# Heads before places within a tile of the output's features, and a new table by slot, in a gated mix of two memory-augmented attentions

## The chip, the cores and the metric

The kernel runs on one core of one Trainium2 chip. The metric is the device time of one execution in microseconds (us). A change of 0.5% or less is treated as no change.

## What is computed

Two independent attentions, A and B, read the same input x (2048 tokens, 640 features), and a gate per token mixes their outputs. Each has 32 heads of 20 features and runs over 4 segments of 512 tokens. Within a segment it is causal softmax attention; between segments it keeps a memory per head (a 20 x 20 matrix M and a vector z). The part of the reference that matters:

```python
def ref(x, wq, wk, wv, wo, beta):          # H = 32, Dh = 20, N = 4, L = 512
    q, k, v = heads_and_segments(x @ wq), heads_and_segments(x @ wk), heads_and_segments(x @ wv)
    g = sigmoid(beta)                      # one number per head
    for s in range(N):
        p = softmax(q[s] @ k[s].T * Dh ** -0.5 + causal_mask)
        a_dot = p @ v[s]
        a_mem = (phi(q[s]) @ M) / (phi(q[s]) @ z + 1e-6)
        o[s] = g * a_mem + (1 - g) * a_dot
        M, z = M + phi(k[s]).T @ v[s], z + phi(k[s]).sum(tokens)
    return concat_heads(o) @ wo

t = sigmoid((x * gate_w).sum(-1))          # one number per token
out = t * ref(x, A...) + (1 - t) * ref(x, B...)
```

All tensors are float32. A product is made of three products with each operand split into a high and a low part (names ending in h and l, or `hi` and `lo`).

## The kernel before, in words

**Tiles and slots.** The work is cut into 8 tiles t: segment t // 2 of attention A (t even) or B (t odd). A tile has 8 groups of 4 heads, so there are 64 groups, and a slot i for each; two more slots end the program. Beside the groups runs the "fill": the projections q, k and v in five blocks of 128 features, and the output product with wo of the tile before.

**Order.** The order on every engine is made when the program is built. A planner keeps a clock, gives each step a cost in us (`put` for an engine, `dma` for a transfer, which all go out on SyncE, the queue SP), and emits a step when its inputs are due by these costs. For a transfer the due time is the issue (0.44), 0.9 us, its own cost, and `lat`. On the chip each engine works its queue in that order and waits where the planner was wrong. The table `RULES` has a row for many of the slots: the order in which the score tiles S (for the row maxima) and T (for the exponentials) are laid between the fill, the share of the slot that they take, and limits on when late steps may come in. A slot without a row keeps the rules of the slot before it.

**A group.** S tiles: TensorE writes a score tile into a bank (line 1205) and VectorE scans it for the row maxima (line 1192, tile `mx`). The maxima are transposed and go into the rows of `qst` beside the queries. T tiles: scores again with the maxima taken off (line 1295), exponentials on ScalarE (line 1287), the mask on GpSimd (line 1288). Then the product with v (line 1315); the result has 32 rows per head: 20 places of the output, and from row 20 on the sum of the exponentials. There are 8 banks, and TensorE waits when the next one is still being read.

**Normalisation.** For tiles 0 to 6 the result of each group is copied (line 1345) and sent to a tensor in memory, `dots[t]` (line 1360), with row 32 h + r for head h. When all eight groups of a tile are there, the tile is read back in another order: five loads of 128 x 512, one per block k of 128 output features (`mix`, line 1434), and one of the sums of exponentials, each repeated for four rows (`reciprocals`, line 1392). VectorE makes the gate over the sum (lines 1375 and 1380); then each of the five is weighed on VectorE (line 1425) or GpSimd (line 1426), whichever has less planned work. For t > 1 the memory part is added (line 1493). High and low parts are made (lines 1416, 1418 and 1419), and the output product may begin. Tile 7 is normalised on the chip.

**The order of features.** A block k of 128 output features holds the places 4 k to 4 k + 3 of all 32 heads. Before, the place is the outer index within a block and the head the inner one. The same order is needed in three other places: the rows of wo, which are brought into it by two passes through memory at the start (`mix_weights`: `wrow`, then `wmix`, line 569; read at line 550), the output tile `O` of the memory part (`by_head`, line 702, written by `mem_unit`, line 898; its columns are transposed at line 921, in `turn`), and `own`, which sums a head's gate over its rows (line 336). For tile 7 the head is outermost over the whole row, before and after.

Of the kernel before, what the change touches and what calls it, by code (L numbers as in the profile page):

```python
# [42 lines left out]
def tile_gated_mix_infini_attn(  # L43
# [282 lines left out]
    def small_tiles():  # L326
# [10 lines left out]
        for i in (2, 3):  # L337
            nc.gpsimd.tensor_tensor(out=own, in0=own, in1=ident[:, H * i:H * i + H], op=ALU.add)
# [1031 lines left out]
    def lanes_of(t):  # L1370
        return dots[t].rearrange("(h r) n -> r h n", r=32)
# [417 lines left out]
```

## Time and profile before

| | |
|---|---|
| median of 3 runs | 1110.36 us (1109.23 to 1113.66) |
| the profiled execution | 1116.47 us, its span 1114.7 us |
| TensorE busy | 1040.0 us, 93% of the span |
| VectorE, ScalarE, GpSimd busy | 772.2, 661.7, 595.4 us |
| mean granted TensorE clock | 0.959 |
| transfers | 241.99 MB, mean 217 GB/s, 149223 packets, 12592 of them under 512 B |

Busy times overlap, so they don't add up to the span. PE is TensorE, PEld its weight loads, DVE VectorE, ACT ScalarE, POOL GpSimd, SPq the queue from which transfers are issued. A row of a group reads: line, engine, operation, written from read, shape, count, busy time, mean of one in ns, idle time just before and what ended it. "DMA row<-dots" is a transfer that writes a row buffer from `dots`. In the chain that ended last a transfer counts from its issue until what waited for it went on.

### The profile page before, as it was taken

The page shows a single profiled execution, that of the slowest core. Times are in us where ns is not written, and L with a number is a line of the kernel's source. Part 1 is how long each engine was busy: PE and PEld are TensorE (multiplying, and loading weights), DVE is VectorE, ACT ScalarE, POOL GpSimd, SP SyncE. Part 2 cuts the span into 40 slices and gives each one's busy share as a digit, 9 for nine tenths or more (in the row PEclk, how much of TensorE's full clock was granted, in tenths as well). Part 3 has the DMA queues.
Part 4 walks back from the last instruction along what each step waited for, and adds up shares of the span by engine and source line. Part 5 has one row for each costly group of instructions (what it writes and reads, how often), then busy time and mean ns, then how long its engine had stood idle before and what let it go on. Part 6 is the DMA issues. An engine that isn't in the chain of part 4 may idle for free.

```text
span 1114.7 us, 30803 instructions
## 1 busy us (share of the span) xinstructions
PE 1040.0 (93%) x11260; PEld 884.7 (79%) x11260; DVE 772.2 (69%) x2605; ACT 661.7 (59%) x1347; POOL 595.4 (53%) x1033
## 2 busy tenths in 40 slices
PE   9899998799979999879997999986999889997998
PEld 7889877678868888778886888886888777876776
DVE  4687776567867678666776877865657677776764
ACT  5376665576645666546764567653766446664572
POOL 4356455556437656465644456455565345654461
PEclk9999999899989999889999999998999889998999
DMA  7999886688667877638776578764866669767522
GB/s 238 293 294 279 263 261 212 185 262 274 230 209 204 260 258 236 204 100 256 233 214 199 165 252 246 249 208 114 252 201 217 197 166 290 221 187 249 143 88 72
DMA packets 149223, 241.99 MB, mean 217 GB/s; under 512 B 12592, under 2 KB 45520, under 8 KB 149072
## 3 DMA queue, kind: packets, MB, share of 16 engines
q1 hardware_dynamic: 149072, 240.03, 70.3%
q8 instruction: 89, 1.46, 0.5%
q14 instruction: 62, 0.51, 0.2%
HBM read 150.83 MB, written 94.65 MB: 220 GB/s over the span
## 4 chain that ended last, share of the span: by engine, by line
PE 73%; DMA 18%; issue 3%; DVE 3%; POOL 1%; ACT 1%; SPq 1%; POOLq 0%; DVEq 0%; ACTq 0%
PE bank L771 42%; PE bank L1315 11%; DMA row<-dots 7%; PE bank L1205 6%; PE bank L1295 6%; DMA row<-in_xT_dram 3%; PE bank L961 3%; DMA wst<-wmix 2%; PE bank L881 2%; PE bank L921 2%; DMA qd<-row 1%; DVE bank L1192 1%; PE bank L1230 1%; DMA kst<-kd 1%; DMA wst<-in_b_wv_dram 1%
## 5 line engine op out<-in xcount | busy, mean ns | idle before, releaser
L1192 DVE CUSTOM_DVE_ANT_0 bank<-bank,tri 128x128 f32<-128x128 f32 (+3 forms) x1024 | 475.1, 521 | 166.9 <-PE bank L1205 130.4
L771 PE MATMUL bank<-row,wh 64*128 64x512 f32 x2308 | 501.7, 404 | 0.2
L1287 ACT ACTIVATE p<-bank 128x512 f32<-128x512 f32 x574 | 314.8, 600 | 149.9 <-PE bank L1295 125.9
L1288 POOL TENSOR_SCALAR_AFFINE_SELECT p<-p 128x256 f32<-128x256 f32 (+1 forms) x574 | 211.6, 377 | 262.4 <-ACT p L1287 243.9
L771 PEld LDWEIGHTS bank<-row,wh 64*128 64x128 f32 x2308 | 322.2, 187 | 11.1 <-DVE O L898 0.6
L771 PE MATMUL bank<-row,wl 64*128 64x512 f32 x1154 | 304.3, 404 | 0.0
L541 POOL TENSOR_TENSOR wl<-wst,wh 128x640 fp32r<-128x640 f32 x115 | 180.1, 1568 | 82.2 <-ACT wh L539 81.6
L771 PE MATMUL bank<-wvh,row 64*128 64x320 f32 x1280 | 199.1, 329 | 8.9 <-DVE row L1493 4.6
L1205 PE MATMUL bank<-kst,qst 60*128 60x128 f32 (+3 forms) x1024 | 185.4, 322 | 19.2 <-DVE row L737 7.0
L1295 PE MATMUL bank<-qst,kst 62*128 62x128 f32 (+3 forms) x1024 | 181.4, 323 | 12.3 <-DVE mx L1192 9.6
L771 PEld LDWEIGHTS bank<-row,wl 64*128 64x128 f32 x1154 | 180.4, 188 | 5.3 <-issue 0.8
L771 PEld LDWEIGHTS bank<-wvh,row 64*128 64x128 f32 x1280 | 161.7, 196 | 12.5 <-DVE row L1493 4.9
L1205 PEld LDWEIGHTS bank<-kst,qst 60*128 60x128 f32 x1024 | 138.3, 190 | 29.4 <-DVE row L737 7.3
L1295 PEld LDWEIGHTS bank<-qst,kst 62*128 62x128 f32 x1024 | 135.0, 189 | 21.4 <-DVE mx L1192 11.0
L1315 PE MATMUL bank<-p,vst 128*32 128x512 f32 (+3 forms) x1904 | 146.5, 431 | 0.5 <-POOL p L1288 0.4
L1192 DVE DVE_READ_ACCUMULATOR2_ANT mx<- 128x1 f32 x1024 | 144.4, 141 | 0.0
L1315 PEld LDWEIGHTS bank<-p,vst 128*32 128x32 f32 x1904 | 58.9, 111 | 87.7 <-issue 65.2
L539 ACT CAST wh<-wst 128x640 fp32r<-128x640 f32 x119 | 87.0, 739 | 57.5 <-DMA wst<-wmix 19.5
L771 PE MATMUL bank<-wvl,row 64*128 64x320 f32 x640 | 110.0, 322 | 0.0
L771 PEld LDWEIGHTS bank<-wvl,row 64*128 64x128 f32 x640 | 87.4, 195 | 0.1
L1345 ACT COPY row<-bank 128x512 f32<-128x512 f32 x60 | 35.3, 589 | 68.9 <-PE bank L1315 63.9
L516 POOL TENSOR_TENSOR wvl<-wst,wvh 128x640 fp32r<-128x640 f32 (+1 forms) x48 | 64.0, 1336 | 21.3 <-ACT wvh L513 20.9
(117 smaller groups left out, 1233.2 us busy)
## 6 DMA issues: line engine op xcount, KB each, us to landing
qst<-qd SPq DMA_DIRECT2D x128, 240.0 KB
kst<-kd SPq DMA_DIRECT2D x128, 240.0 KB
qd<-row SPq DMA_DIRECT2D x40, 512.0 KB
kd<-row SPq DMA_DIRECT2D x40, 512.0 KB
dots<-row SPq DMA_DIRECT2D x56, 256.0 KB
wst<-wmix SPq DMA_DIRECT2D x35, 320.0 KB
row<-dots SPq DMA_DIRECT2D x42, 256.0 KB
qd<-row SPq DMA_DIRECT2D x40, 256.0 KB
```

What stands on the lines that cost most here:

```text
L516: put("G", 0.77 * n, lambda: nc.gpsimd.tensor_tensor(out=wl[:, a:b, :], in0=w3, in1=r32(wh[:, a:b, :]), op=ALU.subtract), end, prio=4)
L539: put("A", 0.625, lambda: nc.scalar.copy(wh, w3), lambda: put(lo_eng, lo_cost, lambda: lo.tensor_tensor(out=wl, in0=w3, in1=r32(wh), op=AL ...
L541: lambda: lo.tensor_tensor(out=wl, in0=w3, in1=r32(wh), op=ALU.subtract), end, prio=3), prio=6)
L771: return nc.tensor.matmul(bank_of, lhsT=w[ROWS[half]], rhs=x_[ROWS[half]], start=start, stop=stop)
L961: return nc.tensor.matmul(b[:, :nh * E1], lhsT=r32(pkn[ROWS[half], P * n:P * (n + 1)]), rhs=vst[t % 2][ROWS[half], n, LO[m] * E1:(HI[m] + ...
L1192: put("D", w / 960.0 + 0.105, lambda: nc.vector.tensor_tensor_reduce(out=sc[:, off:off + w], in0=sc[:, off:off + w], in1=tri[:, L - w:], s ...
L1205: lane_ops[half].append((mm(w), lambda pair=pair, qb=qb, off=off, w=w, r=r, sc=sc: nc.tensor.matmul(sc[:, off:off + w], lhsT=q[r, pair, P ...
L1287: put("A", 0.483, lambda: nc.scalar.activation(pt, sc, AF.Exp, scale=SCALE), lambda: (bank.give(sc), put("G", 0.15 + 0.105 * len(todo), la ...
L1288: "G", 0.15 + 0.105 * len(todo), lambda: nc.gpsimd.affine_select(out=blocks, in_=blocks, pattern=[[0, len(todo)], [1, P]], base=0, channel ...
L1295: lane_ops[half].append((mm(w), lambda pair=pair, kb=kb, off=off, w=w, r=r, sc=sc: nc.tensor.matmul(sc[:, off:off + w], lhsT=k[r, pair, P ...
L1315: nc.tensor.matmul(po[32 * j:32 * j + 32, P * kb:], lhsT=vst[t % 2][:, kb, h * E1:h * E1 + 32], rhs=pts[i, n, f][0][:, off:off + w], start ...
L1345: either(0.483, lambda: nc.scalar.copy(r32(oT), po), 0.605, lambda: nc.vector.tensor_copy(r32(oT), po), end, 2)
```

## The change

Within a block of 128 features the head becomes the outer index and the four places the inner one. So the three kinds of transfer (`dots` loads, sums of exponentials, `wmix` writes) have 32 heads outermost and four places within; the bytes and their number are the same. The memory part writes `O` in runs of four places, `own` is made with a fill and two selections, and the table of rules is replaced as a whole. Lines between the table and `own` stand three earlier than before, lines behind 900 two later (1434 is 1436 now).

```diff
@@ RULES @@
-        2: "TSTSTSTSTS 1.039 2.38 0.30 8 2.8 1.6 0.76",
-        4: "TSTTSSTSTS 1.042 2.38 0.30 4 0.0 1.6 1.57",
...
+        1: "TSTSTSTSTS 0.984 2.38 0.30 4 3.8 1.6 1",
+        2: "TSTTSSTSTS 1.041 2.38 0.30 8 0.0 1.6 1.16",
...
@@ -333,9 +330,12 @@
         for t in kst:
             nc.gpsimd.memset(r32(t), -1.0)
         nc.gpsimd.memset(gate, 0.0)
-        nc.gpsimd.tensor_tensor(out=own, in0=ident[:, :H], in1=ident[:, H:2 * H], op=ALU.add)
-        for i in (2, 3):
-            nc.gpsimd.tensor_tensor(out=own, in0=own, in1=ident[:, H * i:H * i + H], op=ALU.add)
+        nc.gpsimd.memset(own, 1.0)
+        for first, step, sign in ((0, -4, 1), (3, 4, -1)):
+            nc.gpsimd.affine_select(
+                out=own, in_=own, pattern=[[step, H]], base=first,
+                channel_multiplier=sign, compare_op=ALU.is_ge, fill=0.0,
+            )
 
     def idle_step():
         z = qst[0][:, 0, :]
@@ -565,9 +565,9 @@
             at(clk[0] + 3.0, lambda: rows(k + 1) if k + 1 < KT else at(clk[0] + 6.0, lambda: blocks(0)))
 
         def blocks(c):
-            heads = wrow[b].rearrange("k p n -> (k p) n").rearrange("(h e) n -> e h n", e=DH)
+            heads = wrow[b].rearrange("k p n -> (k p) n").rearrange("(h e) n -> h e n", e=DH)
             dma(2.0, lambda: nc.sync.dma_start(
-                out=wmix[b][c].rearrange("(e h) n -> e h n", h=H), in_=heads[4 * c:4 * c + 4]),
+                out=wmix[b][c].rearrange("(h e) n -> h e n", h=H), in_=heads[:, 4 * c:4 * c + 4, :]),
                 (lambda: mixed_there.add(b)) if c == KT - 1 else None, prio=500)
             if c < KT - 1:
                 at(clk[0] + 3.0, lambda: blocks(c + 1))
@@ -699,7 +699,7 @@
     Ot = {}
 
     def by_head(t, o):
-        return o.rearrange("p n (h e) -> p n h e", e=DH) if t == 7 else o.rearrange("p n (e h) -> p n h e", h=H)
+        return o.rearrange("p n (h e) -> p n h e", e=DH) if t == 7 else o.rearrange("p n (c h e) -> p n h c e", c=KT, h=H)
 
     O_store = Store([sb.tile([P, NB, D], F32, tag=f"O{i}", name=f"O{i}", bufs=1) for i in range(2)])
     OTs = {}
@@ -896,8 +896,10 @@
                 out=w, in0=pm[:, :nh, DH], scalar=1e-6, in1=gq[t][:, n, h0:h1], op0=ALU.add, op1=ALU.mult)
             nc.vector.reciprocal(w, w)
             nc.vector.tensor_tensor(
-                out=by_head(t, Ot[t])[:, n, h0:h1, :],
-                in0=pm[:, :nh, :DH], in1=w[:, :, None].to_broadcast([P, nh, DH]), op=ALU.mult,
+                out=by_head(t, Ot[t])[:, n, h0:h1],
+                in0=pm[:, :nh, :DH] if t == 7 else pm[:, :nh, :DH].rearrange("p h (c e) -> p h c e", c=KT),
+                in1=w[:, :, None].to_broadcast([P, nh, DH]) if t == 7 else w[:, :, None, None].to_broadcast([P, nh, KT, DH // KT]),
+                op=ALU.mult,
             )
 
         def end():
@@ -1368,7 +1370,7 @@
             big.want((F32,), lambda y, k=k: mix(t, k, y), prio=2)
 
     def lanes_of(t):
-        return dots[t].rearrange("(h r) n -> r h n", r=32)
+        return dots[t].rearrange("(h r) n -> h r n", r=32)
 
     def reciprocals(t, d, g):
         def gates():
@@ -1390,7 +1392,7 @@
         landed = then_all(2, gates)
         b = t % 2
         dma(0.8, lambda: nc.sync.dma_start(
-            out=r32(d), in_=lanes_of(t)[DH:DH + 1, :, :].to_broadcast([4, H, L])), landed, prio=-1, lat=1.6)
+            out=r32(d), in_=lanes_of(t)[:, DH:DH + 1, :].to_broadcast([H, 4, L])), landed, prio=-1, lat=1.6)
         dma(0.8, lambda: nc.sync.dma_start(
             out=r32(g), in_=rowg[t // 2][NB * b:NB * b + NB, :].rearrange("n p -> (n p)")[None, :].to_broadcast([P, L])), landed, prio=-1, lat=1.6)
 
@@ -1431,7 +1433,7 @@
             else:
                 waiting.setdefault(t, []).append(weigh)
 
-        dma(0.82, lambda: nc.sync.dma_start(out=r32(y), in_=lanes_of(t)[4 * k:4 * k + 4, :, :]), landed, prio=0, lat=1.6)
+        dma(0.82, lambda: nc.sync.dma_start(out=r32(y), in_=lanes_of(t)[:, 4 * k:4 * k + 4, :]), landed, prio=0, lat=1.6)
 
     def fin_ok(i):
         t, u = divmod(i, 8)
```

The order on the queues moves a little nearly everywhere. Two places, both at the end of tile 3. First SP, from the first load from `dots` on; before:

```order
L1392 DMA row_10577_8935<-dots_120 128x1x512
L1394 DMA row_10578_8936<-rowg_125 128x512
L1434 DMA row_10583_8938<-dots_120 128x1x512
L1434 DMA row_10586_8939<-dots_120 128x1x512
L1434 DMA row_10589_8940<-dots_120 128x1x512
L1434 DMA row_10592_8941<-dots_120 128x1x512
L1434 DMA row_10595_8942<-dots_120 128x1x512
L1163 DMA qst_80<-qd_101 60x2x512 x2
L1163 DMA kst_84<-kd_109 60x2x512
L750 DMA qd_101<-row_10660_8987 128x2x512
L750 DMA qd_101<-row_10661_8988 128x512
```

and now:

```order
L1394 DMA row_10574_8941<-dots_120 128x1x512
L1396 DMA row_10575_8942<-rowg_125 128x512
L1436 DMA row_10580_8944<-dots_120 128x1x512
L1436 DMA row_10583_8945<-dots_120 128x1x512
L1436 DMA row_10586_8946<-dots_120 128x1x512
L1436 DMA row_10589_8947<-dots_120 128x1x512
L1436 DMA row_10592_8948<-dots_120 128x1x512
L1165 DMA qst_80<-qd_101 60x2x512 x2
L1165 DMA kst_84<-kd_109 60x2x512
L750 DMA qd_101<-row_10648_8997 128x2x512
L1244 DMA qst_82<-mr_162 2x8x128 x2
L750 DMA qd_101<-row_10649_8998 128x512
```

The seven transfers (sums, gates of the tokens from `rowg`, five blocks) stand together in both, and behind them the quads `qst` and `kst` of the next groups and the projected q (`qd`); one transfer of the row maxima (`qst` from `mr`) has come in between. Second VectorE, from the gate over the sums to the next score scans (shown by their two instructions, an ISA row on the bank and one on `mx`); before:

```order
L1375 SCALAR_TENSOR_TENSOR row_10577_8935<-row_10577_8935,gcol_133,row_10578_8936 128x512
L737 TENSOR_TENSOR row_10661_8988<-bank_137,row_10660_8987 128x512
L1380 RECIPROCAL row_10577_8935<-row_10577_8935 128x256
L727 SCALAR_TENSOR_TENSOR row_10662_8989<-bank_137,row_10662_8989 128x512
L737 TENSOR_TENSOR row_10702_9019<-bank_136,row_10701_9018 128x512
L1380 RECIPROCAL row_10577_8935<-row_10577_8935 128x256
L727 SCALAR_TENSOR_TENSOR row_10703_9020<-bank_136,row_10703_9020 128x512
L1425 TENSOR_TENSOR row_10586_8939<-row_10586_8939,row_10577_8935 128x512
L1425 TENSOR_TENSOR row_10592_8941<-row_10592_8941,row_10577_8935 128x512
L1425 TENSOR_TENSOR row_10595_8942<-row_10595_8942,row_10577_8935 128x512
L1192 ISA bank_137,mx_9080<-bank_137,tri 128x512
L1192 ISA mx_9080 128x1
```

and now:

```order
L1377 SCALAR_TENSOR_TENSOR row_10574_8941<-row_10574_8941,gcol_133,row_10575_8942 128x512
L737 TENSOR_TENSOR row_10649_8998<-bank_138,row_10648_8997 128x512
L1382 RECIPROCAL row_10574_8941<-row_10574_8941 128x256
L720 TENSOR_SCALAR bank_138<-bank_138 128x512
L1382 RECIPROCAL row_10574_8941<-row_10574_8941 128x256
L721 TENSOR_TENSOR row_10650_8999<-bank_138,row_10650_8999 128x512
L1427 TENSOR_TENSOR row_10583_8945<-row_10583_8945,row_10574_8941 128x512
L1427 TENSOR_TENSOR row_10589_8947<-row_10589_8947,row_10574_8941 128x512
L1427 TENSOR_TENSOR row_10592_8948<-row_10592_8948,row_10574_8941 128x512
L1194 ISA bank_139,mx_9068<-bank_139,tri 128x512
L1194 ISA mx_9068 128x1
```

In both three weighings stand between the reciprocal and the scans; one evacuation of a projection less stands before them (L737 and L727 before; L720 and L721 now).

111 rows, old and new, of the table RULES are left out of this document.

## Prediction

> **What bounds the kernel now.** I read the page first, then the busy time of each engine by stretch, then the waits, the timeline of one stall, and the chain of work that ended last.
>
> ```profile
> span 1114.7 us, 30803 instructions
> PE 1040.0 (93%) x11260; PEld 884.7 (79%) x11260; DVE 772.2 (69%) x2605; ACT 661.7 (59%) x1347; POOL 595.4 (53%) x1033
> ```
>
> TensorE is the engine to watch: 93% of the span, and its weight loads lie beside it. 75 us of the span it does nothing. The view by stretch tells where; I put the borders round the slices in which the page shows a lower granted clock. Columns: stretch, length, TensorE busy (instructions), granted clock, share of the 16 DMA engines, GB/s.
>
> ```profile
> 182.00:216.00 34.00, 24.13 (x195) 0.80 0.60 183
> 314.00:339.00 25.00, 17.40 (x163) 0.80 0.64 202
> 453.00:489.00 36.00, 25.29 (x270) 0.76 0.54 163
> 597.00:615.00 18.00, 11.26 (x100) 0.81 0.71 224
> 736.00:772.00 36.00, 24.58 (x270) 0.81 0.59 175
> 875.00:902.00 27.00, 18.23 (x190) 0.68 0.74 216
> 1002.00:1025.00 23.00, 15.10 (x148) 0.85 0.68 219
> sum 199.00, PE 135.99; mean PE 19.43
> ```
>
> ```profile
> 0.00:182.00 182.00, 176.22 (x1885) 1.00 0.87 270
> ...
> 339.00:453.00 114.00, 113.99 (x1285) 1.00 0.80 241
> ...
> 1025.00:1114.70 89.70, 84.66 (x904) 0.97 0.39 117
> sum 915.70, PE 904.02; mean PE 113.00
> ```
>
> The first fence is seven stretches, one for each of the seven tiles whose normalisation goes through `dots`; the second is all the rest. In the rest TensorE stands 11.7 us of 915.7, 10.8 of it before 182 and after 1025 us. In the seven it stands 199.00 - 135.99 = 63.0 us, and there alone the granted clock falls, to 0.68 to 0.85. So nearly all that an order or a transfer could win lies in these 199 us. What happens in the fourth (timeline: start, length, instruction, idle before it and what ended that):
>
> ```profile
> 589.13 8.57 SPq L1434 DMA_DIRECT2D row<-dots  x5
> ...
> 602.21 1.46 DVE L1425 TENSOR_TENSOR row<-row,row 128x512 f32<-128x512 f32 x1
> 607.54 0.69 DVE L1425 TENSOR_TENSOR row<-row,row 128x512 f32<-128x512 f32 x1 [3.88 <-DMA row<-dots]
> 610.15 0.69 DVE L1425 TENSOR_TENSOR row<-row,row 128x512 f32<-128x512 f32 x1 [1.92 <-DMA row<-dots]
> 610.76 0.69 DVE L1192 CUSTOM_DVE_ANT_0 bank<-bank,tri 128x512 f32<-128x512 f32 x1
> ...
> 611.57 0.80 PE L1205 MATMUL bank<-kst,qst 60*128 60x256 f32 x4 [4.79 <-DVE mx L1192]
> ```
>
> Five loads from `dots` are issued; VectorE comes to the weighing of the loaded rows (L1425) before they are there and stands 3.88 and 1.92 us. Behind it in its queue lies the scan of a score tile (L1192). TensorE needs the bank which that scan frees, and stands 4.79 us. VectorE is not the bound; its queue is held by a transfer. The waits in total say the same for GpSimd, and for ACT with two other kinds of transfer:
>
> ```profile
> POOL row L1426 <- DMA row<-dots: 37.0, 9, 8.8
> DVE row L1425 <- DMA row<-dots: 34.1, 10, 6.8
> ...
> ACT wh L539 <- DMA wst<-wmix: 19.5, 4, 13.4
> ...
> ACT row L584 <- DMA row<-in_xT_dram: 17.7, 6, 8.3
> ```
>
> How long the transfers take is in the chain that ended last (its sum by line, cut at the page's width, then start, length, what):
>
> ```profile
> by line: PE bank L771 42.3%; PE bank L1315 11.2%; DMA row<-dots 7.4%; PE bank L1205 5.9%; PE bank L1295 5.9%; DMA row<-in_xT_dram 3.3%; issue 3.0%; PE bank L961 2.7%; DMA wst<-wmix 2.5%; PE bank L881 1.7%; PE bank L921 1.7%; DMA qd<-row 1.4
> ...
> 150.70 8.61 DMA qd<-row
> ...
> 171.81 8.48 DMA row<-dots
> ...
> 439.03 4.70 DMA dots<-row
> ...
> 594.89 15.24 DMA row<-dots
> ...
> 886.51 8.38 DMA row<-dots
> ```
>
> `dots<-row` and `row<-dots` both move 256 KB. The one takes 4.70 us, the other 8.4 to 15.2; seven of them lie on the chain and make 7.4% of it, 82 us, 11.8 us each. They differ in how the transfer is cut: `dots<-row` has 128 rows outermost, `row<-dots` four places outermost and 32 heads within. That the cut makes the difference is my reading; no row tells the number of engines that worked.
>
> **The change, part by part.**
>
> *Transfers with 32 heads outermost* (35 loads L1434, 7 denominators L1392, 10 `wmix` writes L569). How late is a load today? The kernel's own planner puts the weighing 0.44 + 0.9 + 0.82 + 1.6 = 3.8 us behind the issue, and the order on each queue is made for that. At 11.8 us the load is 8.0 us late. Price after the change: from below 4.70 us (same bytes, 128 rows outermost), from above 8.61 us (`qd<-row`, twice the bytes). I take the first, since the bytes are equal, and add the queue behind one another. The first stretch moves 270 GB/s at a share of 0.87, so all engines together 310 GB/s, and 256 KB is 0.85 us of them. They are issued 0.58 us apart:
>
> ```profile
> L1434 SPq DMA_DIRECT2D row<-dots x35: 507/578/3877, 173.0 to 1001.5; - x35
> ```
>
> Each then waits 0.27 us more than the one before it, over seven 0.8 us on average: 5.5 us, 1.7 late instead of 8.0.
>
> What the stalls cost: 63.0 us of standing, and work done at a lower clock, busy time by one minus the clock, stretch by stretch: 4.8 + 3.5 + 6.1 + 2.1 + 4.7 + 5.8 + 2.3 = 29.3 us. Together 92.3 us. If what is left goes with the lateness, 1.7/8.0 = 21% of it stays, a gain of 73 us; if 1.7 us is borne without a stall, as the 4.70 us of `dots<-row` are (planned 3.1, in a stretch where TensorE is busy 113.99 of 114.00 us), all 92 go. I take 80. At the upper price, 4.8 us late, 60% stays and the gain is 37. The late `wmix` and `in_xT` loads lie in the same seven stretches and in the same queue behind the `row<-dots`; I count them with these.
>
> The page "DMA: Bandwidth & Descriptors" of the Trainium skill (section "Why a DMA increments its semaphore by 16 and not by 1") says that a transfer is split over the largest number up to 16 that divides both sides' slowest dimension: that is 4 engines before and 16 after. By it the lower price is the right one, and the gain lies at 80 or above; no row here shows an engine's own queue.
>
> *The clock.* It falls behind short stands too:
>
> ```profile
> 182.50:184.00 1.50, 0.12 (x2) 1.00 0.63 143
> 184.70:188.00 3.30, 3.30 (x20) 0.50 0.28 105
> ```
>
> 1.4 us idle, then 3.3 us of work at half the clock: so a stand that stays also costs 1.7 us of clock, and I let both shrink together. The page "TensorE: Matmul & The Clock Gate" of the Trainium skill (section "Part 1: The HAM clock gate") states an idle window of about 3.4 us before the clock halves. This trace disagrees: 1.4 us was enough. What that rule would do here is a rival below.
>
> *Nothing on the path:* the write of the output tile in runs of four (L898).
>
> ```profile
> 280.00:1000.00 720.00, 31.81 (x44) 0.95 0.71 215
> 1028.00:1040.00 12.00, 1.71 (x4) 1.00 0.62 157
> ...
> PE bank L921 <- DVE O L898: 2.3, 1, 2.3
> ```
>
> 44 writes with scattered places take 31.81 us of VectorE, 0.72 each; four (of the shorter form) with a head's places in a row take 0.43. The new form lies between, or above if a fourth dimension costs: plus or minus 8 us of an engine that is idle 31%, plus or minus 4 on the path, taken as 0. `own` on GpSimd: a fill and two selections for three additions, in a queue that stands 8.57 us right after:
>
> ```profile
> 16.18 1.57 POOL L516 TENSOR_TENSOR wvl<-wst,wvh 128x640 fp32r<-128x640 f32 x1 [8.57 <-ACT wvh L513]
> ```
>
> *The table by slot* moves steps, not work: 9734 instructions on TensorE and 942 transfers on SP in both orders; seven copies of a bank go from ACT to VectorE, some 5 us of 772 if each takes the 0.69 us of L1425's rows above. SP passes the same group of `dots` loads; while these land sooner, the 8.57 us for which it stood over five issues shrink too, and what stands behind (quads, `qd`, `kd`) starts sooner. In the calm stretches the old table left nothing to win, so it can win only what is left in the seven, or lose. I give it plus or minus 8 us and 0 as its value.
>
> **Sum.** The profiled execution took 1116.5 us, of which the span is 1114.7; it lies 6 us above the median of 1110.4. 1116.5 - 80 = 1036.5, scaled by 1110.4/1116.5: 1030.8. I say 1030.
>
> **Rivals.**
>
> *The loads get only half as fast* (1073 us): a burst of seven among `qd`, `kd` and quads lands after 8.6 us because all 16 engines are shared. For it: in the chain `qd<-row` took 8.61. Against: the share in the seven stretches is 0.54 to 0.74, below the 0.87 of the start.
>
> *The change does not reach the transfer* (1110 us): reading `dots` is slow because of its rows 64 KB apart, whichever dimension is outermost. For it: the reads keep these rows. Against: the `in_xT` loads, with no such rows, are late only in the same stretches, so something blocks the queue, not the reading alone.
>
> *The clock falls anyway* (1045 us): the half clock behind short stands has another cause than the stands and stays when they go. Taken as half of the 29.3 us, 15 less to gain. For it: a stand of 1.4 us is short to cause 3.3 us of half clock. Against: 1.00 in the calm stretches. The rule of the Trainium skill's page "TensorE: Matmul & The Clock Gate", Part 1, named above, would lead here.
>
> *The table puts a wait into the calm slots* (slower): the scan on VectorE comes late for the scores.
>
> ```profile
> PE bank L1295 <- DVE mx L1192: 9.6, 4, 3.4
> ```
>
> One such wait is 2.4 us, with its clock 4.1. To eat 80 us it takes 20, one in every third of the 64 slots; with one in every second slot 32 x 4.1 = 131 us, 1161 us. Against: 339 to 453 us without any, and 31% room on VectorE.
>
> *All goes and the table helps* (1008 us): 92.3 + 8 + 2 less.
>
> **How the numbers follow.** Stalls mostly gone 0.73 (1013 to 1052 alone), half as fast 0.10, clock anyway 0.04, all and more 0.07, no effect 0.03, slower table 0.03. The range runs from 1008 (92 and the table's 8 off, rounded) to 1062 (a gain of 48, between the two prices): it leaves out the slow part of "half", the last two, and part of "all and more". Faster by over 0.5% (5.5 us, about what the measurement can tell) holds all but the last two: 0.94; same 0.03; slower 0.03.
>
> **What would show it.** Right: `row<-dots` on the chain at 5 to 6 us each and under 2% in all; waits for it on GpSimd and VectorE under 8 us each, from 37.0 and 34.1; granted clock over 0.98 in what were the seven stretches; TensorE busy over 96%. The `in_xT` and `wmix` waits of ACT fall under 6 us without being changed themselves. Writes L898 under 0.72 us. Wrong: `row<-dots` still over 9 us (the cut was not the cause), or loads at 5 us with TensorE still standing over 30 us in these places (another queue holds it), or stands spread over the calm stretches (the table).

## The result, and the profile after

| | before | after |
|---|---|---|
| median (lowest to highest), 4 runs each | 1112.01 us (1109.23 to 1114.08) | 1023.02 us (1020.24 to 1024.47) |
| ratio, 95% interval | | 0.9198, 0.9167 to 0.9229 |
| the profiled execution, its span | 1116.47, 1114.7 us | 1020.24, 1018.2 us |
| TensorE busy; the rest of the span | 1040.0; 74.7 us | 1000.0; 18.2 us |

The kernel got 89 us faster. The prediction was 1030 us, 1008 to 1062.

The page of after, TensorE's granted clock in tenths by slice, and the packets by size:

```profile
span 1018.2 us, 30838 instructions
...
PE 1000.0 (98%) x11260; PEld 857.4 (84%) x11260; DVE 773.7 (76%) x2611; ACT 659.7 (65%) x1342; POOL 606.0 (60%) x1032
...
PEclk9999999999999999999999999999999999999999
...
DMA packets 148886, 241.99 MB, mean 238 GB/s; under 512 B 13216, under 2 KB 46144, under 8 KB 148416
```

The same bytes, but 624 more packets under 512 B (12592 before). That is 12 more for each of the 52 transfers whose cut changed (35 + 7 + 10). The trace says the same in another way: the semaphore of such a transfer is raised in 5 steps before and in 16 after (worked out from the semaphore updates). The page "DMA: Bandwidth & Descriptors" of the Trainium skill (section "Why a DMA increments its semaphore by 16 and not by 1") says that each engine that takes part raises it by one, and the rest is added at once. 4 + 1 steps for four engines and 16 for sixteen agree with it, and so do 12 more small packets, if an engine writes one each.

The stretches of the seven tiles, laid round the loads of after and as long as the ones of before. Columns: stretch, length, TensorE busy (instructions), granted clock, share of the 16 DMA engines, GB/s.

```profile
170.00:204.00 34.00, 33.05 (x383) 1.00 0.92 297
286.00:311.00 25.00, 23.97 (x309) 1.00 0.89 263
411.00:447.00 36.00, 34.12 (x407) 1.00 0.83 241
543.00:561.00 18.00, 16.68 (x203) 1.00 0.85 268
671.00:707.00 36.00, 35.88 (x453) 1.00 0.79 244
798.00:825.00 27.00, 26.69 (x336) 1.00 0.90 259
908.00:931.00 23.00, 20.93 (x243) 1.00 0.92 291
sum 199.00, PE 191.32; mean PE 27.33
```

```profile
sum 819.20, PE 808.72; mean PE 101.09
```

TensorE stands 7.7 us in the seven, from 63.0, and the clock is full. In the rest (second fence) it stands 10.5 us, from 11.7. The DMA engines' share, 0.54 to 0.74 before, is 0.79 to 0.92.

The fourth stretch again, on the queue SP, VectorE and GpSimd (start, length, instruction, idle before it and what ended that):

```profile
544.20 3.66 SPq L1436 DMA_DIRECT2D row<-dots  x5
...
554.25 3.85 DVE L1427 TENSOR_TENSOR row<-row,row 128x512 f32<-128x512 f32 x3
558.03 0.68 DVE L1194 CUSTOM_DVE_ANT_0 bank<-bank,tri 128x512 f32<-128x512 f32 x1
```

```profile
553.87 2.98 POOL L1428 TENSOR_TENSOR row<-row,row 128x512 f32<-128x512 f32 x2 [2.17 <-DVE row L1382]
```

The five issues take 3.66 us instead of 8.57. VectorE weighs its three rows without a wait, and the scan L1194 follows at once. GpSimd now waits for the gate over the sum (L1382), not for a load. The waits for `dots`, `wmix` and `in_xT` that the view of the waits still lists, in total:

```profile
ACT row L584 <- DMA row<-in_xT_dram: 5.3, 5, 1.7
DVE row L1427 <- DMA row<-dots: 1.5, 1, 1.5
POOL row L1428 <- DMA row<-dots: 0.8, 1, 0.8
```

And the chain that ended last, summed by line:

```profile
by line: PE bank L771 48.3%; PE bank L1317 13.1%; PE bank L1297 7.0%; PE bank L1207 6.7%; PE bank L881 2.8%; PE bank L963 2.5%; PE bank L923 2.0%; issue 1.3%; DMA dots<-row 1.3%; DVE bank L1194 1.1%; DVE row L1420 0.9%; PE bank L1232 0.8%; 
```

`row<-dots`, 7.4% before, is gone from it; 84% of what is left is TensorE's own work.

How long a transfer takes from its issue to its last semaphore update, medians over the trace: the five block loads 11.85 us before and 5.01 after, the loads of the sums 7.67 and 4.11, the `wmix` writes 9.2 and 4.75. Transfers whose cut did not change gained too, in their tails: nine in ten `in_xT` loads landed within 13.0 us before and 6.7 after, the `qst` loads from `qd` within 10.9 and 6.4.

These are times in a burst. In the last tile the load of the sums and the five block loads took 6.1, 8.2, 10.2, 12.6, 14.6 and 14.8 us before, and 3.1, 4.2, 4.3, 4.3, 4.9 and 5.7 after. So much of the 11.85 us is a load's wait for the ones before it: before, each adds about 2 us to the next.

### The profile page after: what moved, and what is told of

It reads as the page before. It is cut to its first block, busy times and chain, and to the rows that moved or that the text cites. A ratio compares the mean times of both kernels' runs of the same rounds, so it can differ in the third digit from the quotient of the medians.

```text
span 1018.2 us, 30838 instructions
## 1 busy us (share of the span) xinstructions
PE 1000.0 (98%) x11260; PEld 857.4 (84%) x11260; DVE 773.7 (76%) x2611; ACT 659.7 (65%) x1342; POOL 606.0 (60%) x1032
## 4 chain that ended last, share of the span: by engine, by line
PE 84%; DMA 6%; DVE 5%; issue 1%; POOL 1%; ACT 1%; SPq 1%; DVEq 0%; ACTq 0%; POOLq 0%
PE bank L771 48%; PE bank L1317 13%; PE bank L1297 7%; PE bank L1207 7%; PE bank L881 3%; PE bank L963 2%; PE bank L923 2%; DMA dots<-row 1%; DVE bank L1194 1%; DVE row L1420 1%; PE bank L1232 1%; DMA kd<-row 1%; DVE row L1427 1%; DMA qd<-row 1%; DMA kst<-kd 1%
## 5 line engine op out<-in xcount | busy, mean ns | idle before, releaser
L1194 DVE CUSTOM_DVE_ANT_0 bank<-bank,tri 128x512 f32<-128x512 f32 (+3 forms) x1024 | 474.4, 519 | 151.5 <-PE bank L1207 118.6
L1290 POOL TENSOR_SCALAR_AFFINE_SELECT p<-p 128x256 f32<-128x256 f32 (+1 forms) x576 | 219.3, 390 | 224.8 <-ACT p L1289 215.6
L771 PEld LDWEIGHTS bank<-row,wh 64*128 64x128 f32 x2308 | 319.7, 185 | 10.9 <-issue 1.2
L771 PE MATMUL bank<-row,wl 64*128 64x512 f32 x1154 | 297.0, 399 | 0.0
L1207 PE MATMUL bank<-kst,qst 60*128 60x384 f32 (+3 forms) x1024 | 177.9, 317 | 4.6 <-DMA kst<-kd 2.8
L771 PE MATMUL bank<-wvh,row 64*128 64x320 f32 x1280 | 179.8, 315 | 1.1 <-DVE mx L1194 1.1
L771 PEld LDWEIGHTS bank<-wvh,row 64*128 64x128 f32 x1280 | 147.9, 185 | 3.0 <-DVE mx L1194 1.3
L1194 DVE DVE_READ_ACCUMULATOR2_ANT mx<- 128x1 f32 x1024 | 143.4, 140 | 0.0
L1317 PE MATMUL bank<-p,vst 128*32 128x256 f32 (+3 forms) x1904 | 142.1, 427 | 0.0
L1207 PEld LDWEIGHTS bank<-kst,qst 60*128 60x128 f32 x1024 | 130.9, 186 | 11.8 <-DMA kst<-kd 2.0
L539 ACT CAST wh<-wst 128x640 fp32r<-128x640 f32 x119 | 86.1, 741 | 31.6 <-PE bank L771 14.6
L771 PE MATMUL bank<-wvl,row 64*128 64x320 f32 x640 | 100.7, 311 | 0.0
L771 PEld LDWEIGHTS bank<-wvl,row 64*128 64x128 f32 x640 | 80.3, 185 | 0.1
L1347 ACT COPY row<-bank 128x512 f32<-128x512 f32 x56 | 33.1, 590 | 64.4 <-PE bank L1317 59.6
```

Source lines behind the costliest of these rows:

```text
L539: put("A", 0.625, lambda: nc.scalar.copy(wh, w3), lambda: put(lo_eng, lo_cost, lambda: lo.tensor_tensor(out=wl, in0=w3, in1=r32(wh), op=AL ...
L771: return nc.tensor.matmul(bank_of, lhsT=w[ROWS[half]], rhs=x_[ROWS[half]], start=start, stop=stop)
L1194: put("D", w / 960.0 + 0.105, lambda: nc.vector.tensor_tensor_reduce(out=sc[:, off:off + w], in0=sc[:, off:off + w], in1=tri[:, L - w:], s ...
L1207: lane_ops[half].append((mm(w), lambda pair=pair, qb=qb, off=off, w=w, r=r, sc=sc: nc.tensor.matmul(sc[:, off:off + w], lhsT=q[r, pair, P ...
L1290: "G", 0.15 + 0.105 * len(todo), lambda: nc.gpsimd.affine_select(out=blocks, in_=blocks, pattern=[[0, len(todo)], [1, P]], base=0, channel ...
L1317: nc.tensor.matmul(po[32 * j:32 * j + 32, P * kb:], lhsT=vst[t % 2][:, kb, h * E1:h * E1 + 32], rhs=pts[i, n, f][0][:, off:off + w], start ...
```

## The experiments

The ratios are to the kernel before on the same chip, with 95% intervals. "Burst" is worked out from the trace: from the issue of a tile's load of sums to the landing of the last of its block loads, mean of seven tiles. It is 30.1 us for before and 16.0 us for after.

### Which part of the change: layout, or table?

The new layout with the old table, and the old layout with the new table. (The first is after with the old `RULES`, the second before with the new; the diff is the one above, its first hunk in the one, all the others in the other.)

> The changed kernel with the table of before: the new order of features alone. If the transfers' cut does it (theory), almost the whole gain is here: 1018 to 1035 us, granted clock over 0.98, TensorE standing under 30 us in all, loads row<-dots at about 5 us. If the new table does it (rival), it stays near 1110 us.

> The kernel before with the new table alone. Theory: the loads still take 8 to 15 us and hold the queues at the end of each tile, so 1095 to 1130 us, granted clock 0.95 to 0.97, since the table cannot shorten a transfer. Rival (the table does it): about 1025 us.

Measured: the layout alone 1026.07 us, ratio 0.9221 (0.9183 to 0.9259), burst 16.6 us. The table alone 1096.80, 0.9857 (0.9816 to 0.9899), burst 28.3 us, and its loads still take 11.2 us (median). The page of the layout alone, and the waits of the table alone:

```profile
PE 1006.9 (98%) x11260; PEld 858.1 (84%) x11260; DVE 774.3 (76%) x2605; ACT 661.1 (65%) x1347; POOL 607.2 (59%) x1033
```

```profile
DVE row L1422 <- DMA row<-dots: 45.4, 13, 7.0
POOL row L1423 <- DMA row<-dots: 35.8, 9, 6.2
```

The layout gives 86 of the 89 us. The table is worth 15 us while loads are late and about 3 when they are not (its interval overlaps that of after, so the 3 are not certain). The waits for the loads did not go with the table (81 us on the two engines, 71 before), and yet TensorE stands 62.6 us in place of 74.7: the order of the rest makes them cost less. The layout alone also shows where the 89 us came from. Of the span's 90.5 us (1114.7 - 1024.2), 33.1 are TensorE busy time (1040.0 - 1006.9, mostly the lower clock) and 57.4 are standing (74.7 to 17.3).

### Is it the number of outermost pieces, or where the data lies?

The old layout and table, with each four-place transfer cut into four of 32 heads. Three kernels: with all three hunks, with the two on `dots`, with the one on `wmix`; what was expected follows in this order.

```diff
-            out=r32(d), in_=lanes_of(t)[DH:DH + 1, :, :].to_broadcast([4, H, L])), landed, prio=-1, lat=1.6)
+        dma(0.8, lambda: [nc.sync.dma_start(
+            out=r32(d)[H * e:H * e + H, :], in_=lanes_of(t)[DH, :, :]) for e in range(4)], landed, prio=-1, lat=1.6)
-        dma(0.82, lambda: nc.sync.dma_start(out=r32(y), in_=lanes_of(t)[4 * k:4 * k + 4, :, :]), landed, prio=0, lat=1.6)
+        dma(0.82, lambda: [nc.sync.dma_start(
+            out=r32(y)[H * e:H * e + H, :], in_=lanes_of(t)[4 * k + e, :, :]) for e in range(4)], landed, prio=0, lat=1.6)
-                out=wmix[b][c].rearrange("(e h) n -> e h n", h=H), in_=heads[4 * c:4 * c + 4]),
+                out=wmix[b][c].rearrange("(e h) n -> e h n", h=H)[e], in_=heads[4 * c + e]) for e in range(4)],
```

> The kernel before, its order of features and its table, but every transfer with four places outermost (loads from dots, sums, wmix writes) goes out as four transfers of 32 heads each, one per place, at the same point of the queue. Theory (it is the outermost dimension of four): the four together land in 5 to 6 us in spite of 156 more issues, and the time is 1020 to 1045 us. Rival (the places of one head 8 KB in a row in the new order, or fewer scattered rows, make the load fast): the load keeps over 9 us and the time stays at 1100 us or more; the issues on SP, 1.7 us more per load, could even make it slower.

> The kernel before with only the loads from dots and the sums cut into four transfers of 32 heads, the ten wmix writes left with four places outermost. Cutting all three gave 1060 us. If the 42 loads at the tile ends carry the loss (theory), 1058 to 1075 us. If the wmix writes matter as much (rival), 1085 us or more.

> The kernel before with only the ten wmix writes cut into four transfers of 32 heads. They lie in calm stretches (118 to 152 and 276 to 304 us), apart from one. Theory: 1105 to 1114 us, no change to tell. Rival (they hold the queue as the loads do): 1090 us or less.

Measured: all three 1059.92 us, 0.9529 (0.9481 to 0.9576), burst 21.3 us; `dots` alone 1057.72, 0.9512 (0.9477 to 0.9547), 21.4 us; `wmix` alone 1109.85, 0.9986 (0.9961 to 1.001). The addresses read and written are those of before; only the cut differs. So 52 to 54 of the 89 us come from the cut alone, and the rows 64 KB apart are not what made the loads slow. The `wmix` writes get faster (2.9 us a piece, median) and no gain can be told. The rival "the change does not reach the transfer" falls here.

What was expected of all three was too low, 1020 to 1045; `dots` alone lies just under its 1058 to 1075, and `wmix` alone in its range. The issues and the waits of that kernel:

```profile
L1434 SPq DMA_DIRECT2D row<-dots x140: 302/419/1514, 172.0 to 953.2; - x140
...
DVE row L1425 <- DMA row<-dots: 8.5, 3, 4.8
POOL row L1426 <- DMA row<-dots: 7.4, 5, 2.7
```

Each piece lands in 2.27 us (median), and the four of a load land 4.03 us after the first issue, sooner than the one transfer of after (5.01). But the queue SP spends 4 x 0.419 us on a load instead of 0.58, so the last piece of a tile is late: 1.1 us more for each load, 6.6 for the six of a tile; the burst is 4.7 us longer than with the layout alone.

### Is it the number of issues?

The new layout (old table), each load cut into four transfers of one place each.

```diff
-        dma(0.82, lambda: nc.sync.dma_start(out=r32(y), in_=lanes_of(t)[:, 4 * k:4 * k + 4, :]), landed, prio=0, lat=1.6)
+        dma(0.82, lambda: [nc.sync.dma_start(
+            out=r32(y).rearrange("(h e) n -> h e n", e=4)[:, e, :], in_=lanes_of(t)[:, 4 * k + e, :]) for e in range(4)], landed, prio=0, lat=1.6)
```

The loads of the sums and the `wmix` writes are cut in the same way.

> The new order of features with the table of before (1026 us), but each load from dots, sum and wmix write goes out as four transfers of 32 heads, one per place: the same number of issues, rows and outermost dimension as in the old order cut by place, which took 1060 us. If what was left there is the price of 156 more issues on SP (theory), 1050 to 1068 us. If the old order of features itself costs something more, such as the scattered writes of the output tile on VectorE (rival), this stays at 1026 to 1036 us.

Measured: 1080.32 us, 0.9727 (0.9688 to 0.9766), burst 24.7 us; expected were 1050 to 1068, so the direction holds and the size was too small. The issues are dearer where the partitions written are four apart:

```profile
L1439 SPq DMA_DIRECT2D row<-dots x140: 447/592/1598, 172.7 to 974.1; - x140
```

0.592 us instead of 0.419: 4 x 0.592 - 0.58 = 1.79 us more per load, against 1.1 in the old layout. The losses over the layout alone are 54 and 34 us. The two ratios agree (1.63 and 1.60), which speaks for the issue time on SP, not the place of the data, as what is left between the four pieces and after.

The same question asked with issues that carry nothing: the layout alone, with three transfers of 64 bytes from `gate_w` to a scratch tensor `junk` behind each block load.

```diff
+            nc.sync.dma_start(out=r32(y), in_=lanes_of(t)[:, 4 * k:4 * k + 4, :])
+            for e in range(3):
+                nc.sync.dma_start(out=junk[j, e:e + 1, :], in_=gate_w[16 * e:16 * e + 16][None, :])
```

> The new order with the table of before (1026 us), and behind each of the 35 loads from dots three more transfers of 64 bytes from gate_w to a scratch tensor: issues without data. If what the cut by place left over is the time of more issues on SP (theory: four of 0.42 us in place of one of 0.58 cost 34 us, four of 0.59 cost 54), these cost 25 to 50 us: 1050 to 1076 us. If it is the smaller pieces or the partitions that they go to (rival), the time stays at 1026 to 1036 us.

Measured: 1136.59 us, 1.023 (1.0179 to 1.028), burst 31.5 us: slower than before, where 1050 to 1076 were expected. SP in the fourth tile:

```profile
600.21 0.58 SPq L1442 DMA_DIRECT2D row<-dots  x1
600.84 1.86 SPq L1445 DMA_DIRECT2D junk<-in_gate_w_dram  x3
602.79 0.57 SPq L1442 DMA_DIRECT2D row<-dots  x1
603.41 3.42 SPq L1445 DMA_DIRECT2D junk<-in_gate_w_dram  x3
...
610.95 0.57 SPq L1442 DMA_DIRECT2D row<-dots  x1
614.01 1.76 SPq L1445 DMA_DIRECT2D junk<-in_gate_w_dram  x3
615.81 0.59 SPq L1442 DMA_DIRECT2D row<-dots  x1
```

The fifth load goes out 15.6 us behind the first, where after issues all five in 3.66. 12 x 0.62 = 7.4 us of it are the issues of the small transfers, and 2.5 those of four loads. In the remaining 5.7 us SP stands, up to 2.49 us in one piece (from 610.95 + 0.57 to 614.01). That piece and one of 1.5 us end when the transfer issued eight places earlier has landed: the program marks its transfers with eight semaphores in turn, and the small ones use these up. The estimate held only the issues. Nor was it an empty load: each of these transfers raised its semaphore in 16 steps and took 6.7 us to land, and the loads beside them 7.28 instead of 4.92. So this run adds more than issues: time of the DMA engines and SP's standing come with them, and it doesn't part the three. That the time between four pieces and one is that of the issues is argued, not shown.

### Fewer pieces than four

Before, with each block load as two transfers of two places each.

```diff
+        dma(0.82, lambda: [nc.sync.dma_start(
+            out=r32(y)[64 * e:64 * e + 64, :], in_=lanes_of(t)[4 * k + 2 * e:4 * k + 2 * e + 2, :, :]) for e in range(2)], landed, prio=0, lat=1.6)
```

> The kernel before with each of the 35 loads from dots as two transfers of two places, so that two is the outermost dimension. If the outermost dimension limits how many engines work (theory), a load takes about twice as long as with four: 18 to 26 us on the chain where it was 11.8, and the kernel is slower, 1180 to 1300 us. If it is the scattered rows (rival), the two halves together take what the whole did and the time is 1100 to 1125 us.

Measured, one run: 1202.66 us, burst 42.6 us. The waits, 37.0 and 34.1 us before:

```profile
POOL row L1426 <- DMA row<-dots: 87.5, 11, 16.8
DVE row L1425 <- DMA row<-dots: 86.5, 12, 12.3
```

Half the bytes in each transfer, yet the halves take 13.5 us (median). The two halves of a load together take 15.1 us (median; 8.8 to 20.0), below the 18 to 26 that were expected, while the time lies in its range. Their semaphores are raised in 3 steps: two engines, by the count above. So more transfers in flight are not what made the kernels with four pieces fast.

### Is it the lateness itself, or that the order did not know of it?

Before, with the planner told how long the loads take: `lat` 9.7 for the block loads and 5.5 for the sums and the gate, from 1.6.

```diff
-        dma(0.82, lambda: nc.sync.dma_start(out=r32(y), in_=lanes_of(t)[4 * k:4 * k + 4, :, :]), landed, prio=0, lat=1.6)
+        dma(0.82, lambda: nc.sync.dma_start(out=r32(y), in_=lanes_of(t)[4 * k:4 * k + 4, :, :]), landed, prio=0, lat=9.7)
```

> The kernel before, transfers untouched, but the planner is told that they land late: lat 9.7 us for the loads from dots in place of 1.6, and 5.5 for the sums and the token gates, as they were measured. The weighings then go behind other work on VectorE and GpSimd. Theory (the loss is the blocked queue, not the length of the transfer in itself): most of the stalls on row<-dots go, TensorE stands 20 to 40 us in place of 69, time 1050 to 1085 us; what is left are the in_xT, wmix and quad loads which wait behind the same transfers. Rival (the output product needs these rows at once, so lateness costs the same wherever it is planned): 1100 us or more.

Measured: 1143.35 us, 1.0268 (1.0224 to 1.0312). The theory falls. The waits for `row<-dots` fell to 4.1 and 1.6 us, and the kernel is slower than before all the same. Its waits, then the fourth tile on SP, ScalarE and TensorE:

```profile
ACT wh L539 <- DMA wst<-wmix: 28.0, 5, 10.9
ACT row L584 <- DMA row<-in_xT_dram: 14.2, 4, 8.8
...
DVE row L1425 <- DMA row<-dots: 4.1, 2, 2.4
```

```profile
605.56 8.96 SPq L1434 DMA_DIRECT2D row<-dots  x5
...
622.37 0.39 SPq L550 DMA_DIRECT2D wst<-wmix  x1
...
632.20 0.72 ACT L539 CAST wh<-wst 128x640 fp32r<-128x640 f32 x1 [10.89 <-DMA wst<-wmix]
...
633.48 0.80 PE L1205 MATMUL bank<-kst,qst 60*128 60x384 f32 x4 [9.75 <-ACT p L1287]
```

A `wmix` load stands behind the five loads in SP's queue, whose issue took 8.96 us; ScalarE's split of it (L539) goes on 9.8 us after its issue and has waited 10.89. The exponential behind it comes late, and TensorE stands 9.75 us. The harm of a slow transfer is not only the wait of its own reader: the transfers next to it are late too, and their readers were not told.

That is one place. It agrees with the standing as a whole, which stays: 77.6 us (1140.4 - 1062.8), from 74.7, where 20 to 40 were expected. It is not what makes the kernel slower than before. TensorE's busy time rose from 1040.0 to 1062.8 us at nearly the same mean clock (0.956, from 0.959): the matmuls' durations add up to 3.846 times the time in which any runs, against 3.939 before, so fewer ran side by side. Nearly all of the 26 us between the two spans is this, and its cause is open. The time lies in the rival's range, but its reason (the output product needs the rows at once) is not tested by it.

The same on the changed kernel: `lat` 2.9 for the three loads, what after's trace shows.

```diff
-... lanes_of(t)[:, 4 * k:4 * k + 4, :]), landed, prio=0, lat=1.6)
+... lanes_of(t)[:, 4 * k:4 * k + 4, :]), landed, prio=0, lat=2.9)
```

> The changed kernel with the planner told what was measured: lat 2.9 us for loads from dots, sums and token gates in place of 1.6, since they land 5.0 us after the issue. If the planner's error is what is left (theory), 5 to 10 us less: 1013 to 1019 us. If later weighings only hold the output product back (rival), 1020 to 1035 us.

Measured: 1061.02 us, 0.955 (0.9519 to 0.9581), 38 us above after. Both theories fall. Its page:

```profile
PE 1037.7 (98%) x11260; PEld 880.3 (83%) x11260; DVE 776.4 (73%) x2610; ACT 662.6 (63%) x1348; POOL 600.1 (57%) x1027
```

TensorE hardly stands more (22.4 us of its span of 1060.1, 18.2 in after), but the same instructions take 38 us longer. About 17 of them are clock (mean 0.984). For the rest, the matmuls' durations add up to 3.905 times the time in which any runs, against 4.008 in after: fewer ran side by side. The loads' burst is 16.1 us, so the loss is not in the loads. Why that order pairs the matmuls worse stays open; the table of rules was written for the old figure, which may be all there is to it.

### The output tile

After, with `O` written in the old scattered way (the memory part is then added to other features than it belongs to; the work is the same).

```diff
-        return ... else o.rearrange("p n (c h e) -> p n h c e", c=KT, h=H)
+        return ... else o.rearrange("p n (e h) -> p n h e", h=H)
```

> The changed kernel with the memory part written into the output tile in the old places (scattered, so the memory part is added to other features than it belongs to; the work is the same). The writes at L898 go back from 0.55 and 0.43 us to 0.81 and 0.59. Theory (off the path): 1020 to 1026 us, no difference. Rival (VectorE's 10 us count): 1028 to 1034 us.

Measured, 5 runs: 1027.82 us (1026.73 to 1031.12), 0.9244 (0.9217 to 0.9271). The write in after, and in this kernel:

```profile
L898 DVE TENSOR_TENSOR O<-bank,mw 128x380 f32<-128x380 f32 x24 | 13.3, 554 | 0.8
L898 DVE TENSOR_TENSOR O<-bank,mw 128x260 f32<-128x260 f32 x24 | 10.3, 429 | 0.8
```

```profile
L898 DVE TENSOR_TENSOR O<-bank,mw 128x380 f32<-128x380 f32 x24 | 19.3, 804 | 0.8
L898 DVE TENSOR_TENSOR O<-bank,mw 128x260 f32<-128x260 f32 x24 | 14.4, 601 | 0.8
```

VectorE saves 10 us, of which the runs show about 5 in the time. That lies between the two expected ranges. The two intervals of the ratio just overlap (0.9217 to 0.9271 and 0.9167 to 0.9229), so a part on the path is likely and not shown.

### One line through the runs

For the kernels with the planner's old figures, burst against time:

| kernel | burst, us | seven bursts over after's, us | time over after's, us |
|---|---|---|---|
| after | 16.0 | 0 | 0 |
| after, scattered output tile | 16.1 | 0 | 5 |
| layout alone | 16.6 | 4 | 3 |
| four pieces, old layout | 21.3 | 37 | 37 |
| the same, `dots` alone | 21.4 | 38 | 35 |
| four pieces, new layout | 24.7 | 61 | 57 |
| table alone | 28.3 | 86 | 74 |
| `wmix` writes alone | 29.7 | 96 | 87 |
| before | 30.1 | 99 | 89 |
| layout and small transfers | 31.5 | 109 | 114 |
| two places | 42.6 | 186 | 180 |

A microsecond by which a tile's loads come later goes with about a microsecond of time, for each of the seven tiles, over the whole range from 0 to 27 us. The two kernels with other planner figures lie off it (burst 29.8 and 1143 us; 16.1 and 1061 us); in both the matmuls ran less side by side (durations of 3.846 and 3.905 times the busy time, 3.93 to 4.01 in the kernels of the table).

## Why the prediction was right, by its steps

*What bounds the kernel, and the cut as the cause.* Right. The seven stretches held the gain: 55.3 of the 56.5 us of standing that went, and the lower clock. The kernels cut into pieces keep the addresses and show the cause, which the prediction had only read from two transfers of one size.

*The time of a load.* Taken as 5.5 us (between 4.70 and 8.61), measured 5.01. Which of its two parts was too high, the single transfer of 4.70 us or the 0.8 us for the queue, differs by tile: the five block loads took 4.2 to 5.7 us in the last and 4.9 to 5.2 in the fourth.

*The gain, 80 of 92.3.* This is the main term that was mis-sized. In the seven stretches 63.0 + 29.3 us were to be had; 7.7 us of standing and no lower clock are left, so 84.6 went. The working had offered as its other end that "1.7 us is borne without a stall, as the 4.70 us of `dots<-row` are", and that end was nearer: the waits for `row<-dots` are 2.3 us in all. The late neighbours, counted "with these", did go with them (no wait for `wmix` is left on the list, 5.3 us for `in_xT`, as announced), and the kernel that was planned late shows that TensorE can stand 77.6 us with only 5.7 us of waits for `row<-dots`.

*The clock, "1.4 us was enough".* Too strong as a rule. After has stands of TensorE of 1.75, 1.31 and 2.07 us and no lower clock behind any of them; the last:

```profile
926.99 0.59 PE L923 MATMUL bank<-ident,O 64*128 64x64 f32 x6 [2.07 <-DVE mx L1194]
```

What decides can be read from the clock records of the traces. In all thirteen kernels the clock changes only at points that lie whole multiples of 3.41 us apart. Counted by these windows, each of the 72 at full clock in which TensorE is busy for less than 45% is followed by one at half clock; of the 3726 with more than 65%, six are; of the 64 between, 29. So the length of one stand does not decide, but how busy a window is in all. The window with the 1.39 us of before and the next one, then the window with the 2.07 us of after and the next one (columns as in the stretches above):

```profile
181.23:184.64 3.41, 2.02 (x20) 1.00 0.71 176
184.64:188.05 3.41, 3.41 (x20) 0.50 0.29 108
```

```profile
923.25:926.67 3.42, 1.67 (x24) 1.00 1.02 228
926.67:930.08 3.41, 3.09 (x47) 1.00 0.76 276
```

Busy for 59 and 49%, both lie between 45 and 65%, where these shares do not tell which way it goes; that stays open. The page "TensorE: Matmul & The Clock Gate" of the Trainium skill (section "Part 1: The HAM clock gate") states an idle window of about 3.4 us. The 3.41 us agree with it. A window idle throughout was not needed here: the one with the 1.39 us was busy for 59% of its time.

The rival that the clock falls anyway (1045 us) is out: the low clock went with the stands. But the full clock throughout is that of the profiled execution; the other three of after have means of 0.994 to 0.996.

*The table, 0 in a range of plus or minus 8.* About -3 with the new layout. Its rival (waits in the calm slots, 1161 us) did not come: 10.5 us of standing outside the seven stretches, from 11.7.

*The output tile, "between, or above".* At the lower end: the shorter form takes 0.43 us, as with a head's places in a row before, and the mean of both is 0.49. Taken as 0 on the path, it gave perhaps 5 us, which are part of what the layout gave.

*The other rivals.* Loads only half as fast (1073 us) would have shown at 8.6 us each; they took 5.01, though the engines' share rose to 0.79 to 0.92 from the 0.54 to 0.74 that were held against this rival. "All goes and the table helps" (1008 us) had both signs right, and the time lies between it and the forecast.

*The sum.* Between the spans of the two profiled executions 96.5 us went (1114.7 - 1018.2), 16.5 more than the 80. They are 4.6 in the seven stretches (84.6 - 80); 2.8 more of lower clock there, since by the clock records TensorE works 64.2 us at half clock, which costs 32.1 and not 29.3; 1.7 for one window at half clock in the last stretch of before; 1.2 of standing outside the seven (11.7 - 10.5); and 6.2 of TensorE busy time that the clock does not account for. Of these 1.0 went with the layout alone and 5.2 between that and after; this may be the table, and is not shown. By medians it is 89 and not 96.5, since before's profiled execution lies 4.5 us above its median and after's 2.8 below.

## What to carry to other kernels

Where a transfer takes two or three times as long as another of the same bytes, look at its outermost dimension before its addresses: here 4 pieces took 11.85 us, 32 took 5.01, and 2 pieces for half the bytes 13.5 (medians, each load in a burst with others). Mend it by the order of the data rather than by more transfers, since each issue costs the queue 0.42 to 0.59 us, and late is late whichever of the two it comes from. Price a late transfer by the whole burst and by its neighbours in the queue, not by its readers' waits alone: telling the planner took the readers' waits away, and TensorE stood as long as before.

## What was not expected of the hardware

- Issues differ in price by the destination's partitions: 0.419 us for 32 partitions in a row, 0.592 for 32 that are four apart, both 64 KB.
- Transfers of 64 bytes are not free: 6.7 us to land among the loads, 16 steps of the semaphore each, and 105 of them, put among the loads, cost 110.5 us (1136.59 against 1026.07), over 1 us each.
- With the loads on time, VectorE and GpSimd weigh at once, and both slow down. The groups of before, then of after:

```profile
L1426 POOL TENSOR_TENSOR row<-row,row 128x512 f32<-128x512 f32 x18 | 22.9, 1275 | 40.3 <-DMA row<-dots 37.0 <-PE bank L921 2.0 <-DVE row L1380 1.3
...
L1425 DVE TENSOR_TENSOR row<-row,row 128x512 f32<-128x512 f32 x17 | 13.4, 799 | 37.3 <-DMA row<-dots 34.1 <-POOL p L1288 3.1
```

```profile
L1428 POOL TENSOR_TENSOR row<-row,row 128x512 f32<-128x512 f32 x17 | 25.3, 1498 | 6.0 <-DVE row L1382 5.0 <-DMA row<-dots 0.8
L1427 DVE TENSOR_TENSOR row<-row,row 128x512 f32<-128x512 f32 x18 | 18.7, 1072 | 1.5 <-DMA row<-dots 1.5
```

From 799 to 1072 ns on VectorE and from 1275 to 1498 on GpSimd: 18 x 0.273 + 17 x 0.223 = 8.7 us of the two engines. In the trace of after the one goes with the other: the eleven instructions of L1427 that lie beside one of GpSimd on two rows (L1428 or L1421) for more than half of their time take 1.27 us on average, the seven that lie beside none 0.76; in before 16 of 17 lie beside none and take 0.76 too. It is also part of what is left on the path. In the fourth tile TensorE stands 1.31 us behind the scan that follows the three weighings, and in the last 2.07 us (the row at 926.99 above); there the three lie on the chain that ended last:

```profile
920.38 4.49 DVE row L1427 x3
```

The page "GPSIMD Engine Reference" of the Trainium skill (section "1. Specifications") says that GpSimd shares its way to SBUF with VectorE, and that an instruction of VectorE with two inputs there contends for it; L1427 is one, and these rows agree.
